# Two products of a channel-mixing layer computed by Strassen's scheme

## The chip, the core and the metric

The kernel runs on one core of one Trainium2 chip. The metric is the device time of one execution in microseconds (us); a kernel's time is the median of its runs.

The engines of the core work side by side, each through its own list of instructions in order, and wait for each other by semaphores. TensorE (PE) multiplies matrices into PSUM, which the kernel uses as 8 banks of 128 x 512 numbers; the loads of its stationary operand are shown as PEld. VectorE (DVE), ScalarE (ACT) and GpSimd (POOL) do elementwise work; POOL gets no PSUM operand here. SyncE (SP) issues the DMAs.

## The reference

Attention with a window and block summaries gives x (2 batches, 768 tokens, 512 channels). Then come two layers. All numbers are float32.

```
def _moe_ref(x, U, V, w_ch1, w_ch2):                 # the first MoE
    h = x.transpose(0, 2, 1) @ U @ V
    u = x + h.transpose(0, 2, 1)
    return u + np.maximum(u @ w_ch1, 0.0) @ w_ch2    # w_ch1 512 x 2048, w_ch2 2048 x 512

def _moe2_ref(x, mu_k, mu_r, w_k, w_v, w_r):         # the second MoE
    x_prev = np.concatenate([zeros, x[:, :-1, :]], axis=1)
    xk = mu_k * x + (1.0 - mu_k) * x_prev
    xr = mu_r * x + (1.0 - mu_r) * x_prev
    k = np.maximum(xk @ w_k, 0.0)                    # w_k 512 x 1024
    v = k * k @ w_v                                  # w_v 1024 x 512
    r = 1.0 / (1.0 + np.exp(-(xr @ w_r)))            # w_r 512 x 512
    return r * v
```

## The kernel before

Every large product runs on PE in the type float32r, with each operand split into a high part (a copy rounded to that type, on ACT) and a low part (the number less its high part, on DVE or POOL). A product is then three matmuls into one bank: high by high, high by low, low by high. So "12 matmuls" below are 4 slices of the contraction x 3.

The weights come as float64 words and are converted on the chip, block by block (128 rows, 512 numbers): `conv_stages` gives nine steps of a block, `load` (SP), `low_words` and `high_words` (ACT), `clamp`, `shift`, `sign` (DVE), `join` (POOL, L407), `high` (ACT, L439), `low` (POOL, L443). There are 54 blocks: 2 for U and V, 16 each for w1 and w2, 8 for wk, 4 for wr, 8 for wv.

The tokens are four chunks of 384 (2 batches x 2). The first part, up to 106 us, attention and the first quarter of the first MoE for batch 0, are an order written out by hand: `ORDER`, a list of step names with numbers that the kernel plays one after the other. A step issues its instructions to their engines, so the list fixes the order within every engine.

After that, generators take over. The first MoE goes by four quarters of its 2048 hidden channels, then chunks, then 4 blocks: `f1` (L483, 12 matmuls of 384 columns), `f2` (L510, 12 matmuls), summed into y (L522). A queue `side` holds jobs of the other engines, above all the conversions of the next weights; `run` takes a job from it at a fixed rate per PE step.

The second MoE, the last 170 us, goes chunk by chunk in `p2_unit`. `prep_jobs` mixes the tokens with their predecessors (L608, L613) and splits them (L619, L624). `k_stage` computes one block of 128 hidden channels: 12 matmuls of 384 columns (L662), relu on ACT (L665), square on DVE (L666), split (L669, L670). `v2_stage`, two blocks later, multiplies the block into three banks, 9 matmuls of 512 columns (L684); with the eighth block the banks are multiplied by the gate (L690, DVE) and stored (L691). `r_stage` computes a gate: 12 matmuls of 512 columns (L646) and a sigmoid (L649), three a chunk. So there are 32 calls each of `k_stage` and `v2_stage` and 12 of `r_stage`. PSUM is two rings of four banks there (`bank`); in `ORDER` the banks are taken and given back one by one (`take`, `give`).

Of the kernel before, what the change touches and what calls it, by code (L numbers as in the profile page):

```python
# [70 lines left out]


# [18 lines left out]
def build(tc, I, out):  # L91
# [241 lines left out]
    def u_stage(n, c):  # L333
        b, d = divmod(n, 4)
        if d == 0:
            u_t[b, c] = (
                pools["u", b].tile([128, KD, CH], F32R, name="uhi", tag="u"),
                pools["u", b].tile([128, KD, CH], F32R, name="ulo", tag="u"),
            )
# [77 lines left out]
    def conv_jobs(blocks, queue=nc.sync):  # L417
        load, *ops = conv_stages(blocks, queue)
        stages = (ops[:2], ops[2:5], ops[5:6], ops[6:7], ops[7:])
        n_blocks = len(blocks)  # L420

        def slot(k):
            if k % 2 == 0 and k // 2 < n_blocks:
                load(k // 2)
            for j in range(len(stages) - 1, -1, -1):
                i, odd = divmod(k - j - 2, 2)
                if not odd and 0 <= i < n_blocks:
                    for op in stages[j]:
                        op(i)

        return [lambda k=k: slot(k) for k in range(2 * n_blocks + len(stages))]
# [16 lines left out]
    def block(nm, f, key, pool, eng=nc_p):
        return (I[nm].bitcast(I32)[f], *put_w(key, pool, eng))

    def quarter_blocks(q, pool):
        res = []
        for i in range(FT):
            f = q * FT + i

            res.append(block("w1", f, ("w1", f), pool, nc_v if q == 0 and i > 1 else nc_p))
            res.append(block("w2", f, ("w2", f), pool))
        return res

# [416 lines left out]
```

## Time and profile before

| | |
|---|---|
| median of 3 runs | 518.05 us (516.36 to 518.37) |
| the profiled execution | 517.4 us |
| its span, first to last instruction | 515.6 us |
| busy PE, DVE, ACT, POOL | 502.8, 320.2, 251.5, 200.6 us |
| granted PE clock | 1.00 throughout (the 2.4 GHz level) |
| moved by DMA | 46.31 MB, mean 90 GB/s |

Span and busy times are of one execution. The matmuls are pipelined: a record's length reaches into the next ones, and what one costs is read from the distance of two starts. PEld is the weight load that belongs to a matmul. A line such as L662 is a line of the kernel above; `bank` is a PSUM bank. "<-" in brackets names what ended an engine's idle time.

### The profile page before, as it was taken

Reading aid. Unit: us, or ns where it says so; the run is one execution under the profiler, and the core shown is the slowest. Engines: PE = TensorE matmul, PEld = TensorE weight load, DVE = VectorE, ACT = ScalarE, POOL = GpSimd, SP = SyncE. Lnnn points to the kernel's source line nnn. Section 1 sums busy time; section 2 is a strip of 40 time slices with the busy share of each in tenths; the row PEclk is TensorE's granted clock in tenths of the full one; section 3 lists DMA queues with packets and bytes.
Section 4 is the critical chain, followed back from the end, with each engine's and each line's share of the span. In section 5 each row is a group of like instructions: output and inputs, shape, how many; then the busy total and the mean of one; then the engine's idle time right before and its main releaser. Section 6 shows DMA issues by size and latency. Waiting matters only on the chain.

```text
span 515.6 us, 8902 instructions
## 1 busy us (share of the span) xinstructions
PE 502.8 (98%) x3468; PEld 467.9 (91%) x3468; DVE 320.2 (62%) x702; ACT 251.5 (49%) x532; POOL 200.6 (39%) x186
## 2 busy tenths in 40 slices
PE   6899999999999999999999999999999999999997
PEld 5578989899999999999999999999878889889885
DVE  6879986458646888368983667476767425343212
ACT  4999866345524454245542546334585424432221
POOL 6547441015634777447783452152621110120000
PEclk9999999999999999999999999999999999999999
DMA  8997651302412333223331230021001001001001
GB/s 312 301 280 228 233 115 49 95 29 95 164 42 81 122 107 102 80 83 123 101 112 73 83 123 1 28 96 47 36 1 61 1 1 63 0 1 38 24 0 61
DMA packets 16329, 46.31 MB, mean 90 GB/s; under 512 B 2704, under 2 KB 4112, under 8 KB 16288
## 3 DMA queue, kind: packets, MB, share of 16 engines
q1 hardware_dynamic: 16112, 45.52, 27.0%
q8 instruction: 27, 0.44, 0.3%
q10 hardware_dynamic: 144, 0.18, 0.1%
q14 instruction: 14, 0.11, 0.1%
q0 software_dynamic: 32, 0.05, 0.0%
HBM read 42.00 MB, written 3.15 MB: 88 GB/s over the span
## 4 chain that ended last, share of the span: by engine, by line
PE 91%; DMA 3%; ACT 2%; DVE 2%; POOL 1%; issue 1%; SPq 0%; DVEq 0%; POOLq 0%
PE bank L510 23%; PE bank L483 22%; PE bank L662 13%; PE bank L684 12%; PE bank L646 5%; PE bank L554 3%; PE bank L578 3%; DMA vt<-vt 2%; PE bank L244 2%; PE bank L289 2%; PE bank L273 2%; PE bank L342 1%; PE bank L311 1%; DMA qt<-qt 1%; PE bank L346 1%
## 5 line engine op out<-in xcount | busy, mean ns | idle before, releaser
L407 POOL TENSOR_TENSOR A<-C,A 128x512 int32<-128x512 int32 (+1 forms) x54 | 70.8, 1310 | 113.3 <-DVE A L401 89.9
L443 POOL TENSOR_TENSOR wlo<-A,whi 128x512 fp32r<-128x512 f32 x50 | 71.3, 1425 | 33.2 <-ACT whi L439 33.2
L510 PE MATMUL bank<-hh,whi 128*128 128x384 f32 x224 | 75.9, 339 | 0.6 <-DVE y L522 0.6
L510 PE MATMUL bank<-hh,wlo 128*128 128x384 f32 x224 | 75.8, 338 | 0.0
L510 PE MATMUL bank<-hl,whi 128*128 128x384 f32 x224 | 75.8, 338 | 0.0
L483 PE MATMUL bank<-uhi,whi 128*128 128x384 f32 x224 | 75.4, 337 | 0.0
L483 PE MATMUL bank<-uhi,wlo 128*128 128x384 f32 x224 | 75.4, 336 | 0.0
L483 PE MATMUL bank<-ulo,whi 128*128 128x384 f32 x224 | 75.4, 336 | 0.0
L490 DVE SCALAR_TENSOR_TENSOR hl<-bank,hh 128x384 fp32r<-128x384 f32 x56 | 31.1, 556 | 67.2 <-ACT hh L488 67.1
L666 DVE TENSOR_TENSOR kt<-kt 128x384 f32<-128x384 f32 x32 | 20.4, 636 | 64.9 <-ACT kt L665 64.9
L488 ACT ACTIVATE hh<-bank 128x384 fp32r<-128x384 f32 x56 | 27.3, 487 | 61.7 <-PE bank L483 61.6
L439 ACT CAST whi<-A 128x512 fp32r<-128x512 f32 x52 | 32.3, 621 | 40.7 <-POOL A L407 40.4
L384 ACT ACTIVATE A<-stg 128x512 f32<-128x512 uint32 (+1 forms) x54 | 36.3, 672 | 29.1 <-DMA stg<-w 16.6
L401 DVE SCALAR_TENSOR_TENSOR A<-stg,A 128x512 int32<-128x512 int32 (+1 forms) x54 | 50.1, 928 | 0.0
L397 DVE TENSOR_SCALAR C<-C 128x512 int32<-128x512 int32 (+1 forms) x54 | 43.6, 808 | 1.7
L662 PE MATMUL bank<-xkl,whi 128*128 128x384 f32 x128 | 43.2, 338 | 0.6 <-POOL xkl L624 0.6
L510 PEld LDWEIGHTS bank<-hh,whi 128*128 128x128 f32 x224 | 42.0, 188 | 1.4 <-ACT C L387 0.9
L662 PE MATMUL bank<-xkh,whi 128*128 128x384 f32 x128 | 43.2, 337 | 0.0
L662 PE MATMUL bank<-xkh,wlo 128*128 128x384 f32 x128 | 43.1, 337 | 0.0
L483 PEld LDWEIGHTS bank<-ulo,whi 128*128 128x128 f32 x224 | 42.1, 188 | 0.0
L483 PEld LDWEIGHTS bank<-uhi,whi 128*128 128x128 f32 x224 | 42.1, 188 | 0.0
L510 PEld LDWEIGHTS bank<-hh,wlo 128*128 128x128 f32 x224 | 42.1, 188 | 0.0
(120 smaller groups left out, 1084.3 us busy)
## 6 DMA issues: line engine op xcount, KB each, us to landing
stg<-w SPq DMA_DIRECT2D x32, 512.0 KB, 3.2
stg<-wk SPq DMA_DIRECT2D x8, 512.0 KB, 3.2
stg<-wv SPq DMA_DIRECT2D x8, 512.0 KB, 3.2
vcat<-vw SPq DMA_DIRECT2D x7, 585.0 KB, 5.3
kt<-kt SPq DMA_DIRECT2D x8, 384.0 KB, 6.2
vt<-vt SPq DMA_DIRECT2D x8, 384.0 KB, 4.7
out<-sig SPq DMA_DIRECT2D x12, 256.0 KB, 2.1
qt<-qt SPq DMA_DIRECT2D x7, 384.0 KB, 6.5
```

What stands on the lines that cost most here:

```text
L384: nc_s.activation(tmp(i, "A"), st[i]["raw"][:, :, 0].bitcast(U32), AF.Copy, scale=2.0 ** -51, bias=2.0)
L397: nc_v.tensor_scalar(out=c, in0=c, scalar1=3, scalar2=None, op0=ALU.logical_shift_left)
L401: nc_v.scalar_tensor_tensor(out=a, in0=st[i]["raw"][:, :, 1], scalar=-2 ** 31, in1=a, op0=ALU.bitwise_and, op1=ALU.bitwise_or)
L407: nc_p.tensor_tensor(out=a, in0=c, in1=a, op=ALU.add)
L439: nc_s.copy(wt[key][0], w)
L443: eng.tensor_tensor(out=lo, in0=w, in1=hi.bitcast(F32), op=ALU.subtract)
L483: nc_t.matmul(ps, w[:, sl], x[:, k], start=(n == 0), stop=(n == 3 * KD - 1))
L488: nc_s.activation(hh, ps, AF.Relu)
L490: lambda: nc_v.scalar_tensor_tensor(out=hl, in0=ps, scalar=0.0, in1=hh.bitcast(F32), op0=ALU.max, op1=ALU.subtract)
L510: nc_t.matmul(acc[d], w[:, sl], x, start=(i == 0 and n == 0), stop=(i == FT - 1 and n == 2))
L662: nc_t.matmul(ps, w[:, sl], x[:, k], start=(n == 0), stop=(n == 3 * KD - 1))
L684: nc_t.matmul(acc, x[:, sl], w, start=(f == 0 and n == 0), stop=(f == KFT - 1 and n == 2))
```

## The change

The products xk @ w_k and k*k @ w_v are computed by Strassen's scheme (in Winograd's form), one level deep. Each operand is cut into 2 x 2 quadrants. For k the cuts go through the hidden channels, the 512 channels of the contraction, and between the two batches; for v through the tokens (the batches), the 1024 hidden channels and the 512 outputs. Seven products of quadrants or sums of quadrants stand for eight. They are numbered 1, 2, 6, 7, 4, 5, 3 in the order in which they run; `LEFT`, `RIGHT` and `RIGHT_X` say which operand each takes ("t" is a scratch quadrant), and the `..._SUMS` tables say how the sums are made, in place.

`k_prod` is one product for one chunk of 384 tokens and one of 4 blocks of 128 hidden channels: 6 matmuls of 384 columns. `k_take` adds its bank to a quadrant z in SBUF (DVE), `k_copy` copies the first one (ACT); product 5 is added twice. `square` and `square_act` do relu and square (one DVE or two ACT instructions, 768 columns). `v_prod` is one product for 128 of 768 rows: 12 matmuls of 256 columns; `v_take` and `v_copy` collect the banks in the same way. Each product needs its operands split anew: a weight quadrant (1024 columns), two pieces of x (768 columns each) or four of z (768 columns each). `gate` multiplies 256 columns, on DVE (`g`) or POOL (`gp`); a store is 128 x 256.

All r products are computed ahead of their use: six (batch 0) before the k products, six (batch 1) after the first two of them.

The generators, `side` and `run` are gone. From the end of `ORDER` on, a second list, `ORDER2` (1198 steps), fixes the order of every engine. Its names: `cl ca cb cc cs cg cp ch co` the nine steps of a conversion; `fa fh fl fb fy yr` the first MoE; `xa xb` mixing; `rh rl ra rs` the gate; `wks xs ms wvs` sums, `wkh xh mh wvh` high parts, `wkl xl ml wvl` low parts; `ka va` products; `kb` to `kg`, `ku` and `vb` to `vg`, `vu` the additions of a product; `q`, `qa` squares; `so` stores. A `p` behind a name puts a step on POOL instead of DVE; the first number of a product is its number in the scheme. The matmuls of the first MoE are the same in number and shape. The blocks of wk and wv are no longer split when converted; `join` writes them into a quadrant. SBUF is laid out by hand in `SLOTS` and `PLACE`; the split parts of z (`mo`) alternate between two pairs of slots.

```diff
+ORDER2 = """
+cl10 fa0.1.0.0 fa0.1.0.1 fh0.1.0.0 cl11 ca10 fl0.1.0.0 cb10 cg10 cc10 fb0.1.0.0 cs10 fh0.1.0.1 cp10 fl0.1.0.1
+cb11 cl12 ca11 cc11 ch10 fa0.1.0.2 cs11 cg11 co10 ca12 cl13 cb12 cg12 fb0.1.0.1 fh0.1.0.2 cp11 fl0.1.0.2 cc12
...
+kr1.2 rlp1.1.2 rl1.1.1 rh1.1.3 ka2.0.0 kr1.3 rl1.1.3 ka2.0.1 kb0.0 wks2 ka2.0.2 kb0.1 ka2.0.3 wksp4 wkh6 kb0.2
+cc51 ka2.1.0 ka2.1.1 kb0.3 ka2.1.2 kb1.0 kb1.1 qa0.0 wkl6 ka2.1.3 ra1.0 kb1.2 xh6.0 kb1.3 xh6.1 cs51 xl6.0
+cp51 wkh7 cg52 ra1.1 rs1.0 xlp6.1 cc50 ra1.2 rs1.1 wklp7 cs50 ra1.3 xh7.0 q0.1 cp50 xh7.1 q0.2 rs1.2 xlp7.0
+ca53 ra1.4 rs1.3 q0.3 cb52 cb53 xlp7.1 ra1.5 cg53 rs1.4 cc52 cs52 ka6.0.0 rs1.5 cc53 cp52 wkh4 cs53 ka6.0.1
+xh4.0 ka6.0.2 kc0.0 cp53 xh4.1 kc0.1 wkl4 ka6.0.3 ka6.1.0 xl4.1 ka6.1.1 kc0.3 kc1.0 ka6.1.2 xl4.0 kc1.1
+ka6.1.3 kc1.2 kc0.2 ka7.0.0 xh5.0 kc1.3 xh5.1 xl5.0 ka7.0.1 wkh5 xlp5.1 kd0.0 ka7.0.2 kd0.1 ka7.0.3 kd0.2
+wklp5 ka7.1.0 kd0.3 ka7.1.1 kd1.0 ka7.1.2 kd1.1 ka7.1.3 kd1.2 ka4.0.0 kd1.3 wkh3 ka4.0.1 xh3.0 ke0.0 wklp3
+xh3.1 ka4.0.2 ke0.1 xl3.1 ka4.0.3 xlp3.0 wvh2 ka4.1.0 ke0.2 ke0.3 ka4.1.1 ke1.0 wvl2 qa1.0 ka4.1.2 ka4.1.3
+ke1.1 mh1.3 ke1.2 ka5.0.0 mh1.2 ml1.3 wvh1 mlp1.2 ke1.3 ka5.0.1 kf0.0 mh1.1 ku0.0 ka5.0.2 kf0.1 mh1.0 ku0.1
+mlp1.1 ka5.0.3 kf0.2 qa1.2 ku0.2 ka5.1.0 kf0.3 ku0.3 mlp1.0 qa1.3 ka5.1.1 kf1.0 ku1.0 ka5.1.2 kf1.1 qa1.1
+wvlp1 ku1.1 ka5.1.3 kf1.2 ku1.2 qa3.0 ka3.0.0 kf1.3 ku1.3 wvsp1 ka3.0.1 kg0.0 mh2.1 ka3.0.2 mh2.0 kg0.1 qa3.3
+ml2.0 ka3.0.3 mlp2.1 ka3.1.0 kg0.2 qa3.1 kg0.3 wvs2 ka3.1.1 qa3.2 wvsp3 ka3.1.2 kg1.1 ka3.1.3 kg1.2 qa2.1
+kg1.0 va1.0 kg1.3 wvs4 qa2.3 va1.1 ms3.1 mh2.3 va1.2 ms3.3 qa2.0 ml2.3 va1.3 mh2.2 ms2.3 va1.4 vr0 ml2.2 qa2.2
+ms3.0 va1.5 vr1 ms2.0 vr4 wvh6 va2.0 ms2.1 vr3 wvl6 vr2 mh6.1 va2.1 mh6.0 vb0 ml6.1 va2.2 mh6.3 vb1 vr5 ml6.0
+wvh7 va2.3 g0.1 ms3.2 so0.1.0 va2.4 ms2.2 ml6.3 mh6.2 va2.5 g0.0 ml6.2 so0.0.0 mh7.3 vb3 va6.0 wvl7 mh7.0
+mh7.1 ml7.3 va6.1 mh7.2 vc0 ml7.0 va6.2 wvh4 ml7.2 va6.3 vb2 g0.3 gp0.2 vb5 so0.3.0 vc1 va6.4 gp0.5 vc2
+so0.2.0 vb4 ml7.1 so0.5.0 gp0.4 va6.5 vc3 vc4 wvl4 so0.4.0 va7.0 mh4.1 ms4.3 mh4.0 mlp4.1 va7.1 vc5 mh4.2 vd0
+ml4.0 mh4.3 va7.2 wvh5 ml4.2 va7.3 ml4.3 va7.4 ms1.0 vd2 va7.5 vd1 ms1.1 vd4 va4.0 mh5.0 ms1.2 mh5.1 vd5 va4.1
+wvl5 mh5.2 wvh3 ml5.1 va4.2 ml5.2 va4.3 ml5.0 ms1.3 va4.4 ms4.2 mh5.3 ve0 va4.5 ml5.3 gp1.0 ve1 va5.0 vd3
+mh3.2 gp1.1 ve2 so1.0.0 ms4.0 mh3.3 so1.1.0 va5.1 ml3.3 mh3.0 ml3.2 va5.2 ms4.1 va5.3 ve3 mh3.1 wvl3 va5.4
+ml3.0 ml3.1 va5.5 ve4 vf1 gp1.4 vf0 va3.0 vu1 gp3.1 so1.4.0 ve5 vu0 gp3.0 so1.1.1 vf3 va3.1 g3.3 gp1.5 so1.0.1
+vu3 so1.3.1 vg0 g1.2 so1.5.0 va3.2 vf2 so1.2.0 g1.3 gp3.2 vf4 so1.3.0 vu4 va3.3 gp3.4 vg1 so1.2.1 vu2 vg2
+so1.4.1 g2.0 va3.4 g2.1 so0.0.1 vg3 so0.1.1 g2.2 gp2.3 vf5 so0.2.1 va3.5 vu5 gp3.5 vg4 so0.3.1 gp2.4 so1.5.1
+vg5 so0.4.1 g2.5 so0.5.1
+"""
...
+SLOTS = {
+    "back": {
+        "A": 3072, "B": 3072, "C": 2048, "U0": 3072, "U1": 3072, "V0": 3072, "V1": 3072, "Y0": 3076
+    },
+    "m": {"D": 4096, "E": 2048, "F": 2048, "Y1": 3076, "R1": 1024, "X1": 1152, "X2": 1536},
+    "n": {"N0": 4096, "N1": 2048, "N2": 1024},
+}
...
+for _p, _n in enumerate((1, 2, 6, 7, 4, 5, 3)):
+    for _i in range(4):
+        PLACE[f"mo{_n}{_i}"] = (("U1", "V0", "Y0", "U0")[_p % 2 * 2 + _i // 2], 1536 * (_i % 2), 1536, 1)
...
+    homes = {tag: (back, n, tag) for tag, n in SLOTS["back"].items()}
+    homes.update({f"H{i}": (h_p, 2 * CH, "h") for i in range(3)})
+    homes.update({f"S{i}": (st_p, 1024, "stg") for i in range(2)})
+    now = {}
+
+    def at(name, n=0, k=0, dt=F32):
+        tag, o, size, *wide = PLACE[name]
+        kind = F32R if wide else F32
+        if tag not in now or now[tag][1] != kind:
+            pool, cols, shared = homes[tag]
+            now[tag] = pool.tile([128, cols], kind, name=tag, tag=shared), kind
+        n = n or size
+        t = now[tag][0][:, o + k * n:o + (k + 1) * n]
+        return t if dt == kind else t.bitcast(dt)
 
...
+            if len(blocks[i]) == 2:
+                to = blocks[i][1]().bitcast(I32)
+                c, a = (t.rearrange("p (h c) -> p h c", h=2) for t in (c, a))
+                del st[i]
+            else:
+                to = a
+            nc_p.tensor_tensor(out=to, in0=c, in1=a, op=ALU.add)
 
...
+    LEFT_SUMS = (((2, 2, 3), ALU.add), (("t", 3, 0), ALU.subtract), ((0, 0, 2), ALU.subtract), ((1, 1, "t"), ALU.subtract))
+    RIGHT_SUMS = (
+        ((0, 1, 0), ALU.subtract), (("t", 3, 0), ALU.subtract), ((1, 3, 1), ALU.subtract), ((2, 2, "t"), ALU.subtract)
+    )
+    X_SUMS = (((1, 1, 0), ALU.subtract), ((0, 0, "t"), ALU.add), (("t", 3, 1), ALU.subtract), ((2, 2, 0), ALU.subtract))
+    LEFT = {1: 0, 2: 1, 6: "t", 7: 0, 4: 3, 5: 2, 3: 1}
+    RIGHT = {1: 0, 2: 2, 6: "t", 7: 1, 4: 2, 5: 0, 3: 3}
+    RIGHT_X = {1: 0, 2: 2, 6: 0, 7: "t", 4: 2, 5: 1, 3: 3}
+
...
+    def sums(eng, table, j, part, *key):
+        places, op = table[j - 1]
+        o, x, y = (part(*key, i) for i in places)
+        eng.tensor_tensor(out=o, in0=x, in1=y, op=op)
+
+    def split_high(dst, src):
+        nc_s.copy(dst[0], src)
+
+    def split_low(eng, dst, src):
+        eng.tensor_tensor(out=dst[1], in0=src, in1=dst[0].bitcast(F32), op=ALU.subtract)
+
...
+    def k_prod(p, c, f):
+        held = k_t[p, c, f] = take()
+        whi, wlo = pair(f"wk{p}")
         n = 0
+        for k in range(2):
+            xhi, xlo = (x[:, c * CH:(c + 1) * CH] for x in x_pair(p, k))
+            sl = slice(f * 256 + k * 128, f * 256 + (k + 1) * 128)
+            for w, x in ((whi, xhi), (whi, xlo), (wlo, xhi)):
+                nc_t.matmul(held[0][:, 0:CH], w[:, sl], x, start=(n == 0), stop=(n == 5))
                 n += 1
+
+    def k_take(p, to, add, last, c, f):
+        held = k_t[p, c, f]
+        z, old = (at(f"z{i}{f}")[:, c * CH:(c + 1) * CH] for i in (to, add))
+        nc_v.tensor_tensor(out=z, in0=held[0][:, 0:CH], in1=old, op=ALU.add)
+        if last:
+            give(held)
+
+    def k_copy(c, f):
+        held = k_t[1, c, f]
+        nc_s.copy(at(f"z1{f}")[:, c * CH:(c + 1) * CH], held[0][:, 0:CH])
+        give(held)
+
+    def square(i, f):
+        z = at(f"z{i}{f}")
+        nc_v.scalar_tensor_tensor(out=z, in0=z, scalar=0.0, in1=z, op0=ALU.max, op1=ALU.mult)
+
+    def square_act(i, f):
+        z = at(f"z{i}{f}")
+        nc_s.activation(z, z, AF.Relu)
+        nc_s.activation(z, z, AF.Square)
+
+    def v_prod(p, s):
+        held = v_t[p, s] = take()
+        whi, wlo = pair(f"wv{p}")
+        n = 0
+        for f in range(4):
+            xhi, xlo = (x[:, s * 128:(s + 1) * 128] for x in pair(f"mo{p}{f}"))
+            sl = slice(f * 256, (f + 1) * 256)
+            for x, w in ((xhi, whi), (xlo, whi), (xhi, wlo)):
+                nc_t.matmul(held[0][:, 0:256], x, w[:, sl], start=(n == 0), stop=(n == 11))
+                n += 1
+
+    def v_copy(s):
+        nc_s.copy(at(f"o1{s}"), v_t[1, s][0][:, 0:256])
+        give(v_t[1, s])
+
+    def o_part(i, s):
+        return at(f"o{i}{s if i else s % 2}")
+
+    def v_take(p, to, add, last, s):
+        held = v_t[p, s]
+        nc_v.tensor_tensor(out=o_part(to, s), in0=held[0][:, 0:256], in1=o_part(add, s), op=ALU.add)
+        if last:
+            give(held)
+
+    def gated(b, s, d):
+        return at(f"sig{b}", DM, s)[:, d * 256:(d + 1) * 256]
+
+    def gate(eng, i, s):
+        t = gated(*((0, s, 0), (1, s, 0), (0, s, 1), (1, s, 1))[i])
+        eng.tensor_tensor(out=t, in0=o_part(i, s), in1=t, op=ALU.mult)
+
+    def store(b, s, d):
+        nc.sync.dma_start(out=out[b, s * 128:(s + 1) * 128, d * 256:(d + 1) * 256], in_=gated(b, s, d))
...
+    steps.update({
+        "fa": f1, "fh": relu_high, "fl": relu_low, "fb": f2, "fy": y_sum, "yr": y_rest,
+        "xa": mix_first, "xb": mix_second, "rh": mix_high, "ra": r_stage, "rs": r_sig,
+        "wkh": lambda p: split_high(*wk_split(p)), "wvh": lambda p: split_high(*wv_split(p)),
+        "xh": lambda *a: split_high(*x_split(*a)), "mh": lambda *a: split_high(*z_split(*a)),
+        "ka": k_prod, "kr": k_copy, "q": square, "qa": square_act, "va": v_prod, "vr": v_copy, "so": store,
+    })
+    for nm, *how in (("b", 2, 0, 1, 1), ("c", 6, 2, 1, 1), ("d", 7, 3, 2, 1), ("e", 4, 1, 3, 1), ("f", 5, 3, 3, 0),
+                     ("u", 5, 2, 2, 1), ("g", 3, 2, 2, 1)):
+        steps["k" + nm] = lambda *a, how=how: k_take(*how, *a)
+        steps["v" + nm] = lambda *a, how=how: v_take(*how, *a)
+    both("rl", mix_low)
+    both("wks", lambda e, j: sums(e, LEFT_SUMS, j, w_part, "wk"))
+    both("wvs", lambda e, j: sums(e, RIGHT_SUMS, j, w_part, "wv"))
+    both("xs", lambda e, j, k: sums(e, X_SUMS, j, x_part, k))
+    both("ms", lambda e, j, k: sums(e, LEFT_SUMS, j, z_part, k))
+    both("wkl", lambda e, p: split_low(e, *wk_split(p)))
+    both("wvl", lambda e, p: split_low(e, *wv_split(p)))
+    both("xl", lambda e, *a: split_low(e, *x_split(*a)))
+    both("ml", lambda e, *a: split_low(e, *z_split(*a)))
+    both("g", gate)
+    play(ORDER2)
```

## Rows read from the trace of the kernel before

**Rows 1.** The page: busy us (share of the span) and instructions of each engine.

```profile
PE 502.8 (98%) x3468; PEld 467.9 (91%) x3468; DVE 320.2 (62%) x702; ACT 251.5 (49%) x532; POOL 200.6 (39%) x186
```

**Rows 2.** The page: shares of the chain that ended last, by engine, by line.

```profile
PE 91%; DMA 3%; ACT 2%; DVE 2%; POOL 1%; issue 1%; SPq 0%; DVEq 0%; POOLq 0%
PE bank L510 23%; PE bank L483 22%; PE bank L662 13%; PE bank L684 12%; PE bank L646 5%; PE bank L554 3%; PE bank L578 3%; DMA vt<-vt 2%; PE bank L244 2%; PE bank L289 2%; PE bank L273 2%; PE bank L342 1%; PE bank L311 1%; DMA qt<-qt 1%; PE bank L346 1%
```

**Rows 3.** Stretches: us, busy PE, PEld, DVE, ACT, POOL, granted clock, DMA.

```profile
340.90:511.60 170.70, 170.13 (x829) 150.08 (x827) 78.27 (x128) 70.41 (x138) 29.19 (x23) 1.00 0.07 24
200.00:250.00 50.00, 50.00 (x287) 49.77 (x286) 34.72 (x52) 21.17 (x39) 30.08 (x25) 1.00 0.28 95
```

**Rows 4.** The chain in order of time: start, us, engine, line, instructions.

```profile
443.21 2.08 PE bank L662 x12
...
500.58 2.12 PE bank L662 x12
502.70 2.10 PE bank L684 x9
504.80 2.79 PE bank L646 x12
```

**Rows 5.** Groups by line, shapes apart: count, busy us, mean ns, idle before.

```profile
L662 PE MATMUL bank<-xkh,whi 128*128 128x384 f32 x128 | 43.2, 337 | 0.0
...
L684 PE MATMUL bank<-whi,hh 128*128 128x512 f32 x96 | 37.9, 395 | 0.0
...
L522 DVE TENSOR_TENSOR y<-bank,y 128x384 f32<-128x384 f32 x48 | 23.3, 548 | 0.0
```

**Rows 6.** PE and its weight loads in order of time: start us, us, instruction.

```profile
60.41 0.60 PE L273 MATMUL bank<-ident,P 128*120 128x128 f32 x4
...
300.16 0.34 PE L483 MATMUL bank<-uhi,whi 128*128 128x384 f32 x1
300.17 0.19 PEld L483 LDWEIGHTS bank<-ulo,whi 128*128 128x128 f32 x1
300.34 0.34 PE L483 MATMUL bank<-ulo,whi 128*128 128x384 f32 x1
```

**Rows 7.** Line L273: durations in ns, smallest, median, largest.

```profile
L273 PE MATMUL bank<-ident,P x96: 270/273/466, 7.3 to 94.9; 128*120 128x128 f32 x96
```

**Rows 8.** DVE in order of time.

```profile
192.57 1.94 DVE L522 TENSOR_TENSOR y<-bank,y 128x384 f32<-128x384 f32 x4
...
356.60 0.69 DVE L401 SCALAR_TENSOR_TENSOR A<-stg,A 128x512 int32<-128x512 int32 x1
357.20 0.42 DVE L391 TENSOR_SCALAR C<-C 128x512 f32<-128x512 f32 x1
...
359.85 1.38 DVE L666 TENSOR_TENSOR kt<-kt 128x384 f32<-128x384 f32 x1 [0.19 <-ACT kt L665]
...
408.15 0.56 DVE L666 TENSOR_TENSOR kt<-kt 128x384 f32<-128x384 f32 x1 [1.99 <-ACT kt L665]
...
409.77 0.55 DVE L624 TENSOR_TENSOR xrl<-xt,xrh 128x384 fp32r<-128x384 f32 x1
```

**Rows 9.** POOL in order of time.

```profile
359.51 1.31 POOL L443 TENSOR_TENSOR wlo<-A,whi 128x512 fp32r<-128x512 f32 x1 [0.73 <-ACT whi L439]
...
402.41 1.01 POOL L624 TENSOR_TENSOR xkl<-xt,xkh 128x384 fp32r<-128x384 f32 x1 [4.96 <-ACT xkh L619]
409.75 1.44 POOL L624 TENSOR_TENSOR xrl<-xt,xrh 128x384 fp32r<-128x384 f32 x1 [6.33 <-ACT xrh L619]
```

**Rows 10.** DMA issues on SP's queue, and the last gates on DVE.

```profile
2.59 0.92 SPq L161 DMA_DIRECT2D kt<-kt  x2
...
510.43 2.15 DVE L690 TENSOR_TENSOR sig<-bank,sig 128x512 f32<-128x512 f32 x3 [5.40 <-PE bank L684]
511.15 1.79 SPq L691 DMA_DIRECT2D out<-sig  x3
```

More of the change, by code (lines that the diff above doesn't have):

```diff
@@ L73, in mask_const @@
+for _i in range(6):
+    PLACE[f"o0{_i}"] = (("E", 1792, 256), ("N2", 768, 256))[_i % 2]
+    PLACE[f"o1{_i}"] = ("E", 256 * _i, 256)
+    PLACE[f"o2{_i}"] = ("C", 256 * _i, 256)
+    PLACE[f"o3{_i}"] = ("F", 768 + 256 * _i, 256) if _i < 5 else ("E", 1536, 256)
 def mask_const():
@@ L335, in u_stage @@
         if d == 0:
[L336 to L339, printed above, removed]
+            u_t[b, c] = [
+                at(f"u{b}{c}", KD * CH, i, F32R).rearrange("p (k c) -> p k c", k=KD) for i in range(2)
+            ]
         ps, _ = ps_t["U", n, c] = take()
@@ L372, in load @@
             src = blocks[i][0]
-            t = (st_p if not wide or i % 3 else x_p).tile([128, 1024], I32, name="stg")
+            if i % 3 == 0 and i < 10:
+                t = x_p.tile([128, 1024], I32, name="stg")
+            else:
+                t = st_p.tile([128, 1024], I32, name="stg", tag="stg")
             p, n = src.shape
-            queue.dma_start(out=t[0:p, 0:n], in_=src)
+            nc.sync.dma_start(out=t[0:p, 0:n], in_=src)
             st[i] = {"raw": t[0:p, 0:n].rearrange("p (n w) -> p n w", w=2), "pn": (p, n // 2)}
@@ L412, in low @@
         def low(i):
-            blocks[i][2](st.pop(i)["A"])
+            blocks[i][2](st[i]["A"])
         return load, low_words, high_words, clamp, shift, sign, join, high, low
[L417 to L431, printed above, removed]
@@ L448, in block, with quarter_blocks @@
[L448 to L458, printed above, removed]
+        return I[nm].bitcast(I32)[f], hi_part, lo_part
+    def quarter_blocks(q, area):
+        return [
+            block(
+                nm, q * FT + i, *(f"{area}{4 * i + 2 * j + k}" for k in range(2)),
+                nc_v if q == 0 and i > 1 and nm == "w1" else nc_p,
+            )
+            for i in range(FT) for j, nm in enumerate(("w1", "w2"))
+        ]
@@ L503, in f2 @@
-        acc = acc_t[q, b, c]
+            acc_t[q, b, c] = [take() for _ in range(KD)]
         for d in range(KD):
-            if d == 2:
-                hold[0] = i == FT - 1
-                yield
             sl = slice(d * 128, (d + 1) * 128)
@@ L642, in r_stage @@
+    def r_stage(b, s):
+        held = r_t[b, s] = take()
+        c, o = divmod(s * 128, CH)
         n = 0
@@ L812, in build @@
-    drain(side)
-    for n, (b, c) in enumerate(chunks):
-        gen = p2_unit(b, c)
-        if n == 0:
-            next(gen)
-            ffn_flush()
-        if n == 0:
-            side.extend(conv_jobs([block("wr", k, ("wr", k), wb_p) for k in range(KD)]))
-        if n + 1 < len(chunks):
-            side.extend(prep_jobs(*chunks[n + 1], mix))
-        run(gen, 1.3 if n == 0 else 0.7)
-        drain(side)
-    while waiting:
-        v2_stage(*waiting.popleft())
+        first_blocks += quarter_blocks(q, ("wa", "wb")[q % 2])
```

402 lines of the change are left out of this document (179 added, 223 removed), and 9 rows, old and new, of the table PLACE.

## The prediction

> **What bounds the kernel now.** I read the page's busy shares first: TensorE (PE) is busy 98% of the span, VectorE (DVE) 62%, GpSimd (POOL) 39% [rows 1]. A busy PE is not yet a bound, so the chain of waits comes next: 91% of the chain that ended last is PE, and the lines of the k product (L662, 13%) and the v product (L684, 12%) have the shares that they have of the work [rows 2]. The table by stretches says the same of the place that changes: from 340.9 to 511.6 us, where r, k and v are computed, PE is busy 170.1 of 170.7 us at full granted clock (1.00, the 2.4 GHz level), while DVE is busy 78.3 and POOL 29.2 [rows 3]. So here every matmul taken off PE is worth its spacing, as long as nothing else becomes late; and the other engines have room, DVE about half.
>
> A matmul's record (337 ns for 384 columns, 395 for 512) overlaps its neighbours [rows 5], so it is not the price. The price is the distance from start to start: the chain gives 12 matmuls of L662 in 2.08 to 2.12 us (174.5 ns each), 9 of L684 in 2.10 us (233 ns), 12 of L646 in 2.79 us (232.5 ns) [rows 4]. Both are 0.454 ns a column.
>
> **Matmuls removed and added.** k before: 4 chunks x 8 blocks x 12 = 384 matmuls of 384 columns, three groups of 128 [rows 5]. k after: `k_prod` has 2 x 3 matmuls, 7 products x 2 chunks x 4 blocks = 56 calls, 336 matmuls of the same width. 48 x 174.5 ns = 8.4 us less.
>
> v before: 288 of 512 columns, three groups of 96 [rows 5], 67.1 us at 233 ns. v after: `v_prod` has 4 x 3 matmuls, 7 x 6 = 42 calls, 504 of 256 columns. No row shows 256 columns. In proportion it is 256 x 0.454 = 116 ns. From below the nearest row is the transposes of L273, 128 columns with a new weight tile each: four take 0.60 us, one record is 0.273, so they are 109 ns apart although half as much streams [rows 6, 7]; there the weight load is what spaces them, and every one of the 504 has a load of the same size. From above the nearest row is 384 columns, 174.5 ns. The load can lie under the stream: the load for the next matmul starts with the matmul before it (300.17 beside 300.16), and the next matmul starts 0.18 us on [rows 6]. I take 116 ns, which is just above the 110: 58.5 us, 8.6 less than before (55.4 and 87.9 at the two ends: 11.7 less or 20.8 more).
>
> That load speaks against the change, and so does the Trainium skill. "TensorE: Matmul & The Clock Gate", section "The mechanism", says that a weight load overlaps a running matmul only when the two use different row groups; here all use the whole array. By that rule and the page's estimate of 107 ns for a 128-column load, load and stream would add up to about 213 ns, 504 of them 107 us, and the v products would be 40 us slower. The rows of 384 columns disagree: by the rule they would be some 267 ns apart, and are 174.
>
> PE alone: 515.6 - 8.4 - 8.6 = 498.6 us of span. The r products (144 matmuls) and the first MoE keep their matmuls.
>
> **What it puts on the other engines.** Prices are again from start to start. DVE: four PSUM additions of 384 columns take 1.94 us with the last record at 0.55, so 0.465 each; a 512-column operation on SBUF 0.60 (L401 at 356.60, next at 357.20) [rows 8]. The slope gives 0.33 for 256 columns, 0.87 for 768, 1.14 for 1024. POOL: 1.01 for 384 columns, 1.31 for 512 when it runs first [rows 9], so 0.72 for 256, 1.9 for 768, 2.5 for 1024.
>
> The second thing the traces show is that POOL and a DVE operation with two SBUF inputs exclude each other. L666 takes 0.56 us alone; started at 359.85 behind a POOL subtraction that ran from 359.51 for 1.31, it took 1.38, the rest of POOL's time and then its own [rows 8, 9]. It goes the other way too: at 409.75 POOL's 1.01 became 1.44, with DVE's 0.55 inside it. DVE additions from PSUM (L522) are not stretched: mean 548 ns over all 48 [rows 5].
>
> Now the counts from ORDER2, by stage. *Stage v (va1.0 to the end), PE 42 x 12 x 0.116 = 58.5 us.* DVE: 42 `v_take` x 0.33 = 13.9 and one k addition 0.5 (PSUM); 21 low parts and 16 sums x 0.87 = 32.2; 5 weight low parts and 1 sum x 1.14 = 6.8; 10 gates x 0.33 = 3.3. Together 56.7 us, 97% of PE's time. POOL: 14 gates x 0.72 + one low part 1.9 = 12.0 us, in which 42.3 of DVE's 56.7 us may not run. If half of POOL's time falls beside PSUM additions or waits, DVE needs 62.7: 4.2 us more than PE's 58.5. *Stage k after ra1 (ka6 to ka3), PE 41.9 us.* DVE 31.2, of which 21.9 from PSUM; POOL 26.2. Sum 57.4; if 60% of the PSUM part lies beside POOL, 44.3, 2.4 over. Inputs of a product are made about one product (8.4 us) ahead here, so this lag costs PE nothing at first, but stage v takes it over. *Stage ra0 to ra1 (50.2 us)*: DVE 25.0, POOL 28.8, sum 53.8 less the overlap of 5.6 us of PSUM additions: even, and with a lead of several us before ka6 needs its parts.
>
> Why lag in stage v reaches PE: the halves `mo` of a product lie in one of two slots, so `mh7` (ACT) and `ml7` (DVE) can't begin before va2 has ended, and all four must be ready when va6 has, 8.4 us later, the first matmul of a product wanting f=0 and its twelfth f=3. Four low parts are 3.5 us of DVE; the list puts up to 5 us of additions, sums and weight parts between them. DVE runs in order: a low part that is late holds the `v_take` behind it, and these hold PSUM banks. At va1 to va2 it is closest, since `mh2.2`, `mh2.3` need the slot that ka3 reads, and squares on ACT (`qa`, two passes) stand before them.
>
> I charge 5 us in all for PE waiting in stage v (bounds 0, if the additions always fall beside POOL, and 16: all of POOL's 12.0 on top of DVE, 68.7 - 58.5 = 10.2, the 2.4, and some 3 us of waits at product changes).
>
> **Edits at nothing.** The conversions of the weights keep their count (54 blocks), only their order moves; 16 blocks lose `ch` and `co`, and their POOL time becomes the sums. In the first MoE, PE was fully busy with the old side jobs (50.00 of 50.00, DVE 34.7, POOL 30.1 from 200 to 250: 65 us of the two in 50) [rows 3]; by the prices above the new list gives DVE 8 to 10.5 us and POOL 9 to 13 in each chunk of 16.7 us of the second and third quarter, about the same, so I cost it at 0, and at most 2 us if a low part of h comes behind a POOL operation. The tail: three gates at the end take 2.15 us and three stores follow [rows 10]; after, one addition, one gate, a half-size store, but POOL's last gate may stand before it: 0, or 1 either way. The stores become 24 on SP's queue, 16 of them in va3; two issues of a load take 0.92 us there [rows 10], so 16 are 7.4 of 8.4 us: 0, unless the gates come in a bunch at the end (1 us).
>
> **Sum.** 498.6 + 5 = 503.6 us of span. The profiled execution took 517.4 us for a span of 515.6, so 1.8 around it; 505.4. The median of the runs is 518.05, 0.65 above that execution: 506.
>
> **Rivals.**
> (a) *All of it is kept.* DVE's additions hide beside POOL and PE never waits: 498.6 + 1.8 + 0.6 = 501, or 498 at 110 ns a matmul. For it: the first MoE already runs DVE and POOL at 65 of 50 us together with PE full [rows 3]. Against: there the products of an engine are wanted tens of us later, here within one product. 0.2.
> (b) *Most is given back.* DVE sets the pace of stage v and its lag from stage k comes on top, 10 to 16 us of waits: 511 to 517. For it: 97% load on an in-order engine that also waits for ACT and PE. 0.16.
> (c) *Slower: the weight load shows.* Place: the 504 matmuls of `v_prod`. If the load needs more than the stream of 256 columns hides, the spacing rises; the change breaks even at 116 + 17.0/504 = 150 ns. At the 174.5 ns of 384 columns v costs 87.9, span 528.0, time 530; with load and stream one after the other (110 + 116) 114 us, time about 556. For it: 110 ns where half as many columns stream, 6 ns under my price. Against: the same share of 9% above a column per cycle at 384 and 512 columns, which no load bound would give. 0.09.
> (d) *It doesn't do what it says*, because the second MoE wasn't bound by PE: excluded by 170.1 of 170.7.
>
> **How the numbers follow.** Mine 0.55 (502 to 510), (a) 0.2, (b) 0.16, (c) 0.09. Half a per cent, 2.6 us, is about what a measurement of this kernel can tell from no change. Faster by more than that (below 515.4): mine, (a), and most of (b), 0.85, less something for delays that I can't see in a list of 1198 steps: 0.82. Within: 0.08. Slower: (c), 0.10. The range reaches to the far end of (a) and through (b): 498 to 517, leaving out (c) and some 8 in 100 more at its two ends.
>
> **What would show it.** PE's matmul count falls from 3468 to 3468 - 48 + 216 = 3636. Twelve matmuls of 256 columns stand 1.39 us apart in the chain; 1.8 or more would be (c). The k calls of six stand 1.05 us apart. In stage v DVE is busy above 90% by records, PE shows waits of 0.5 to 2 us at product changes (va1 to va2 above all), put down to DVE's low parts, and DVE's two-input records are stretched where POOL runs. No such waits is (a); waits inside products, on banks, is (b). The prediction is wrong if PE waits appear in the first MoE or at ka6.

## The result: 499.5 us, and the profile after

The changed kernel takes 499.5 us (median of 4 runs, 498.3 to 500.9) where the kernel before takes 518.2 (4 runs beside it): a ratio of 0.9648, 95% interval 0.9613 to 0.9682. I had predicted 506, with 498 to 517 as the range. The direction is right; the 5 us that I let DVE take back are not there, and what came is the rival in which all of it is kept (501).

The profiled execution has a span of 498.1 us. The page's first part (busy us, share, instructions), answering to [rows 1]:

```profile
PE 484.7 (97%) x3636; PEld 464.1 (93%) x3636; DVE 401.4 (81%) x790; ACT 276.2 (55%) x532; POOL 252.3 (51%) x203
```

3636 matmuls, as counted. DVE, POOL and ACT do 81, 52 and 25 us more. The page's shares of the chain that ended last, answering to [rows 2]:

```profile
PE 79%; DVE 10%; ACT 6%; DMA 3%; issue 1%; SPq 0%; DVEq 0%
```

PE's share fell from 91 to 79%, and DVE has 10%, ACT 6%. The chain in order of time (start, us, line, instructions) says where; it answers to [rows 4]. L707 is r, L772 `k_prod`, L804 `v_prod`; L742 are low parts, L739 high parts and L736 sums; L778 and L816 are the additions of k and v, L793 and L794 the two passes of `square_act`, L825 the gates, L828 the stores. The letters are slots of SBUF.

```profile
341.94 16.79 PE bank L707 x72
358.74 16.80 PE bank L772 x96
375.54 16.78 PE bank L707 x72
392.32 18.89 PE bank L772 x108
...
415.83 0.85 ACT H L794
416.69 1.46 ACT V L739 x2
...
439.71 0.96 DVE U L742
440.67 0.88 DVE B L736
...
483.10 1.81 DVE U L742 x2
...
485.39 8.73 PE bank L804 x72
```

r and the first k products run on PE without a break: 96 matmuls of 384 columns in 16.80 us are 175 ns each. From 415.0 to 439.7 us the chain goes through ACT's squares and high parts, from 439.7 to 485.4 through DVE, and then it returns to PE. A chain that runs through ACT and DVE says that they were just in time or late. They were late at one place: the only wait of PE above 0.2 us after the first part of the program is at 485.4, at the first matmul of va3 (engine, line, what it waited for: us, times, longest us):

```profile
PE bank L804 <- DVE E L816: 0.5, 1, 0.5
```

The stretches of stage k (after the second r), of the first product of stage v, and of all of stage v, answering to [rows 3] (length, then busy PE, PEld, DVE, ACT, POOL, granted clock, DMA):

```profile
391.90:434.00 42.10, 42.10 (x242) 42.02 (x241) 38.52 (x61) 27.90 (x35) 29.47 (x14) 1.00 0.00 1
...
434.20:442.60 8.40, 8.40 (x74) 8.40 (x73) 8.07 (x11) 8.30 (x13) 0.38 (x1) 1.00 0.00 0
...
434.10:494.10 60.00, 59.50 (x505) 59.14 (x503) 58.84 (x95) 29.18 (x40) 14.02 (x16) 1.00 0.13 45
```

In stage v DVE is busy 58.8 of 60.0 us and PE 59.5: a tie. In its first product ACT is tied too, with 8.3 of 8.4 us. The price of 256 columns, which no row of before had, from PE in order of time:

```profile
489.71 0.86 PE L804 MATMUL bank<-N,U 128*128 128x256 f32 x6
490.41 0.87 PE L804 MATMUL bank<-N,V 128*128 128x256 f32 x6
491.12 0.86 PE L804 MATMUL bank<-N,U 128*128 128x256 f32 x6
```

Twelve take 491.12 - 489.71 = 1.41 us, 117.5 ns each; 504 of them 59.2 us. Last, the end, answering to [rows 10]:

```profile
494.15 0.42 DVE L816 TENSOR_TENSOR C<-bank,C 128x256 f32<-128x256 f32 x1 [0.57 <-PE bank L804]
...
494.61 0.42 DVE L825 TENSOR_TENSOR V<-C,V 128x256 f32<-128x256 f32 x1
494.65 0.81 SPq L828 DMA_DIRECT2D out<-V  x2
```

One addition, one gate, a store: from PE's last matmul to the end 4.0 us, as before.

Where the 17.5 us of span came from, by the starts of PE's lines in the two traces (a k call that the kernel before runs ahead of its last `f2` is counted to the second MoE): the first part (to the first `f1` matmul) 106.3 before, 107.3 after; the first MoE 236.7 and 234.6, 2.1 won; the second MoE 168.6 and 152.2, 16.4 won; the tail 4.0 and 4.0. The 1.0 us lost in the first part can't be put down to the change: its steps are the same in the changed kernel and in all the runs below, and in these twelve traces it ends anywhere from 105.8 to 110.3 us.

### The profile page after: what moved, and what is told of

It reads as the page before. It is cut to its first block, busy times and chain, and to the rows that moved or that the text cites. A ratio compares the mean times of both kernels' runs of the same rounds, so it can differ in the third digit from the quotient of the medians.

```text
span 498.1 us, 9378 instructions
## 1 busy us (share of the span) xinstructions
PE 484.7 (97%) x3636; PEld 464.1 (93%) x3636; DVE 401.4 (81%) x790; ACT 276.2 (55%) x532; POOL 252.3 (51%) x203
## 4 chain that ended last, share of the span: by engine, by line
PE 79%; DVE 10%; ACT 6%; DMA 3%; issue 1%; SPq 0%; DVEq 0%
PE bank L595 24%; PE bank L618 23%; PE bank L772 7%; PE bank L707 7%; PE bank L640 4%; PE bank L663 4%; DMA vt<-vt 3%; PE bank L370 2%; PE bank L415 2%; DVE U L742 2%; PE bank L399 2%; PE bank L804 2%; PE bank L467 1%; DVE N L742 1%; DVE V L742 1%; PE bank L437 1%
## 5 line engine op out<-in xcount | busy, mean ns | idle before, releaser
L605 DVE SCALAR_TENSOR_TENSOR h<-bank,h 128x384 fp32r<-128x384 f32 x56 | 30.9, 552 | 45.0 <-ACT h L600 44.7
L600 ACT ACTIVATE h<-bank 128x384 fp32r<-128x384 f32 x56 | 27.4, 488 | 68.1 <-PE bank L595 68.1
L519 DVE TENSOR_SCALAR C<-C 128x512 f32<-128x512 f32 (+1 forms) x54 | 43.7, 810 | 3.3 <-POOL A L541 2.0
L515 ACT ACTIVATE C<-stg 128x512 f32<-128x512 f32 (+1 forms) x54 | 36.2, 673 | 7.6 <-POOL N L541 5.6
L804 PE MATMUL bank<-N,U 128*128 128x256 f32 x252 | 35.9, 280 | 0.5 <-DVE E L816 0.5
L618 PE MATMUL bank<-h,D 128*128 128x384 f32 x192 | 35.9, 336 | 0.0
L618 PEld LDWEIGHTS bank<-h,D 128*128 128x128 f32 x192 | 33.5, 188 | 0.0
L393 ACT ACTIVATE P<-P,nm 128x120 f32<-128x120 f32 x96 | 29.6, 385 | 6.9 <-DVE nm L382 6.7
L804 PEld LDWEIGHTS bank<-N,U 128*128 128x128 f32 x252 | 32.5, 188 | 0.7 <-issue 0.7
L618 PE MATMUL bank<-h,B 128*128 128x384 f32 x144 | 27.2, 337 | 0.0
L707 PE MATMUL bank<-N,U 128*128 128x512 f32 x108 | 27.1, 395 | 0.0
L707 PEld LDWEIGHTS bank<-N,U 128*128 128x128 f32 x108 | 20.2, 188 | 4.7
L804 PE MATMUL bank<-N,V 128*128 128x256 f32 x144 | 21.0, 282 | 0.0
```

Source lines behind the costliest of these rows:

```text
L515: nc_s.activation(tmp(i, "C"), st[i]["raw"][:, :, 1].bitcast(F32), AF.Abs)
L519: nc_v.tensor_scalar(out=c, in0=c, scalar1=as_float(0x38000000), scalar2=as_float(0x47EFFE00), op0=ALU.max, op1=ALU.min)
L605: nc_v.scalar_tensor_tensor(out=hl, in0=held[0][:, 0:CH], scalar=0.0, in1=hh.bitcast(F32), op0=ALU.max, op1=ALU.subtract)
L618: nc_t.matmul(acc_t[q, b, c][d][0][:, 0:CH], w[:, sl], x, start=(i == 0 and n == 0), stop=(i == FT - 1 and n == 2))
L707: nc_t.matmul(held[0], xr(c, i)[:, k, o:o + 128], w, start=(n == 0), stop=(n == 3 * KD - 1))
L804: nc_t.matmul(held[0][:, 0:256], x, w[:, sl], start=(n == 0), stop=(n == 11))
```

## The experiments

All are the changed kernel with one thing altered, and stand against its 499.5 us (499.49 where it was run again, beside the run with both sets of matmuls and the one without POOL's gates). The kernel before took 518.1 to 518.2 beside each of them. "..." marks a cut in the code.

**Put the k matmuls back.** 49 of the 56 k calls repeat their last matmul.

```diff
+        last = 5 if (c, f) == (1, 3) else 6
...
+        if last == 6:
+            nc_t.matmul(held[0][:, 0:CH], wlo[:, sl], xhi, start=False, stop=True)
```

> Of the 48 matmuls that the k products lost, 49 are put back: each of 49 of the 56 k calls gets a seventh matmul of 384 columns, a repeat of its last one, so its sum holds that term twice. Nothing else moves. Theory 1, PE sets the time in stage k and the fewer matmuls are the gain: 49 x 174.5 ns = +8.5 us, 508.0 from 499.5. Theory 2, the gain of the k products came from somewhere else, the new list or the removed squares on the old path: PE has hidden room in stage k and the time stays within 2 us of 499.5. Rival with the engines tied: DVE, busy 38.3 of 41.9 us there, gets the extra 8.5 us as slack, so stage v starts with its low parts further ahead and the time grows by 7.5 at most 8.5.

Measured 508.8 us, +9.3 (507.2 to 509.8). In the traces it is 83.9 us from the first k matmul to the last, against 75.3, with the second r between them: +8.6, against the 8.5 of the first theory. PE sets the time there.

**Put the v matmuls back.** Two more in 36 of the 42 v calls.

```diff
+        last = 13 if s < 5 or p == 1 else 11
...
+        for _ in range(last - 11):
+            nc_t.matmul(held[0][:, 0:256], xhi, wlo[:, sl], start=False, stop=(n == last))
+            n += 1
```

> 72 matmuls of 256 columns are put back into the v products: two more, repeats of the last one, in 36 of the 42 calls, so these sums hold that term three times; 576 x 256 columns are the 288 x 512 of before. Theory 1, PE sets the time in stage v: 72 x 117 ns = +8.4 us, 507.9. Theory 2, DVE sets the pace in stage v (it is busy 59.1 of 60.3 us there) and PE runs in its shadow: the first extra microsecond of PE is free and the rest is not, +7 to +7.5 us, 507; if DVE were the bound by more than its busy time shows, much less, 500 to 503.

507.6 us, +8.1, and PE's one wait is gone. The runs (506.6 to 509.5) can't tell the theories' +8.4 from +7.5. The traces can: from the first v matmul to the last it is 67.6 us in place of 59.7, +7.8, which is 72 matmuls at 117.5 ns (8.5) less the 0.6 us that PE had lost in stage v to waits. PE was the bound there too, DVE not above it by more than that.

**Both at once**, with the changed kernel run again beside it.

> The changed kernel as it is, as the base for the other two runs of this call: 498 to 501 us.

> Both sets of matmuls are put back at once (49 of 384 columns into the k products, 72 of 256 into the v products, each a repeat of a term that the sum then holds more than once), with all else of the change left in. Theory 1, the fewer matmuls of PE are the gain of the second MoE, and the rest of the gain is the first MoE's (236.7 to 234.6 us of span): 8.6 + 8.4 = +17.0, so 516.5 if the base is 499.5, some 2 us below the kernel before. Theory 2, one of the two hides in room that the other makes: +10 to +14, 510 to 514.

499.49 and 516.1 us: +16.6. This kernel has the new list, Strassen's sums and all the added work of DVE, POOL and ACT, and PE streams as many columns as before the change (384 more): it is 0.9953 of the kernel before (0.9933 to 0.9973). In the traces its second MoE is 16.4 us longer than that of the changed kernel, which is all that the change had won there. So nearly the whole gain is the matmuls, and the remaining 2.1 us are as much as the first MoE won in the trace.

**Double seven DVE operations in stage v.**

```diff
-... ml2.3 ... ms2.3 ... ml6.1 ... ml7.3 ... ml4.0 ... ml5.1 ... ml3.3 ...
+... ml2.3 ml2.3 ... ms2.3 ms2.3 ... ml6.1 ml6.1 ... (and so on)
```

> Seven DVE operations of 768 columns in stage v are done twice (six low parts and one sum, the same values written again): 7 x 0.87 = 6.1 us more DVE work, none of it a product's last input. Theory 1, PE alone sets stage v and DVE has room: 0 to +1 us, 499.5 to 500.5. Theory 2, the two are tied at 98%: DVE has 60.3 - 59.1 = 1.2 us left, the rest shows: +4.5 to +6 us, 504 to 505.5. The charge in my prediction (DVE 4 to 5 us over PE) would need the full 6.1, 505.6.

506.5 us, +7.0 (505.6 to 510.1). In the stretch of stage v DVE is busy 65.5 of 66.5 us, and PE waits five times, for 4.3 us, three times for DVE and twice for a high part of ACT:

```profile
452.68 0.38 PE L804 MATMUL bank<-N,V 128*128 128x256 f32 x1 [0.84 <-ACT V L739]
...
453.90 1.25 PE L804 MATMUL bank<-N,V 128*128 128x256 f32 x5 [0.83 <-DVE V L742]
...
492.00 0.96 PE L804 MATMUL bank<-N,U 128*128 128x256 f32 x6 [1.61 <-DVE E L816]
```

Every microsecond of the 6.1 showed: the tie is real, DVE has nothing to spare. In the trace the second MoE is 6.6 us longer, and DVE's busy time in stage v grew by as much; the rest of the +7.0 is within the spread of the runs. The mean granted clock of that stretch is 0.97, where it was 1.00.

**Leave out 12 sums.**

```diff
-... ms3.1 ... ms3.3 ... ms1.0 ... ms4.2 ...    (all ms1, ms3, ms4)
```

> 12 of the 16 sums of z are left out (all but zt = z3 - z0), so the v products take other operands than the scheme wants; 12 x 0.87 = 10.4 us of DVE work less in stage v. Theory 1, PE sets stage v and DVE is tied with it: only the waits of PE go, 0.3 + 0.6 us of 60.3, so 498.6 to 499.5. Theory 2, DVE paces stage v by more than PE's idle shows: 494 to 497.

498.0 us, 1.5 less. DVE is busy 47.0 us in this stretch, and PE all of it:

```profile
434.20:492.60 58.40, 58.40 (x500) 58.40 (x499) 47.03 (x82) 28.09 (x40) 13.44 (x15) 1.00 0.14 47
```

12 us less work on DVE buy 1.5, of which the trace shows 0.7 in stage v (from the first v matmul to the last 59.0 us for 59.7): DVE's excess over PE was no more than that.

**Move POOL's gates to DVE, and leave them out.** The first changes `gp` to `g` in the list, the second deletes the 14 steps.

> The 14 gates of POOL run on DVE, at the same place of the list: 14 x 0.33 = 4.6 us more on DVE, and POOL has only one operation left in stage v (1.9 us). If POOL's 12 us cost DVE half of themselves, as I charged, DVE wins 5 or 6 us back and the time stays at 499.5. If they cost it 2.4 us (59.1 busy less the 56.7 of the sum), DVE needs 59.1 + 4.6 - 2.0 = 61.7 of 60.3: +1 to +2.5 us, 500.5 to 502.

> The 14 gates of POOL are left out, so 14 of the 24 output blocks are not multiplied by r. DVE's list stays as it is, and POOL has 1.9 us of work in stage v in place of 12. If POOL blocked DVE for half of its time, DVE would win 5 us and PE would lose its last waits: 498 and DVE busy about 54 us in stage v. If POOL's gates ran beside DVE's additions from PSUM, 498.5 to 500 and DVE busy 57 to 59.

On DVE: 503.9 us, +4.4, with 4.6 us of work moved; stage v grew by 1.3 us in the profiled execution and the tail by 2.2. (That execution is the longest of the four, 506.4 us; 3.0 of its excess lie in the first part.) Left out: 499.3 us. The stretch of stage v without POOL's gates, of the same length as the one of after:

```profile
433.00:493.00 60.00, 59.48 (x505) 59.11 (x503) 58.76 (x96) 29.17 (x40) 2.65 (x2) 1.00 0.14 47
```

POOL is busy 2.65 us in place of 14.0, and DVE 58.76 in place of 58.84. So POOL's gates cost DVE 0.1 us. Both of my expectations for the move to DVE missed: I had still credited it with 2 us or more of blocking taken away, and there was next to none to take.

**Double seven DVE low parts in stage k.**

```diff
-... wkl4 ... xl4.1 ... xl4.0 ... xl5.0 ... xl3.1 ... ml1.3 ... ml2.0 ...
+... wkl4 wkl4 ... xl4.1 xl4.1 ... (and so on)
```

> The same dose in stage k, ka6 to ka3: seven low parts on DVE are done twice, six of 768 columns and one of 1024, 6.4 us more. DVE is busy 38.3 of 41.9 us there, part of it waiting for POOL. Theory 1, inputs are a product ahead, so the lag is absorbed: 0 to +1 us, 500. Theory 2, the lag is handed on to stage v, which has about 1 us to spare: 6.4 - 3.6 - 1.2 = +1.6 us or more, 501 to 503; with POOL in the way of the longer DVE list up to +6, 505.

511.8 us, +12.3, with seven runs from 508.9 to 516.3: nearly twice the 6.4 us of the dose, and beyond both theories. The reason is in two views of this run. DVE and then POOL in order of time:

```profile
402.50 4.82 DVE L742 TENSOR_TENSOR U<-A,U 128x768 fp32r<-128x768 f32 x2
...
435.36 5.37 DVE L742 TENSOR_TENSOR Y<-H,Y 128x768 fp32r<-128x768 f32 x2
```

```profile
401.63 1.85 POOL L742 TENSOR_TENSOR Y<-V,Y 128x768 fp32r<-128x768 f32 x1 [4.19 <-ACT Y L739]
403.43 3.07 POOL L742 TENSOR_TENSOR C<-N,C 128x1024 fp32r<-128x1024 f32 x1
...
434.98 1.85 POOL L742 TENSOR_TENSOR Y<-H,Y 128x768 fp32r<-128x768 f32 x1
436.80 3.12 POOL L736 TENSOR_TENSOR D<-D 128x1024 f32<-128x1024 f32 x1
```

Two low parts that take 1.82 us alone take 4.82 and 5.37 where POOL is running. The list was in step: POOL's operations lay for the most part beside DVE's additions. Pushed out of step, four of the doubled low parts wait 10.0 us in all for POOL, where the four single ones waited 0.8. PE then waits 3.3 us in stage k and 4.7 in stage v. The first wait leaves its clock at 1.00; behind two waits that end at 449.8 and 450.8 (1.9 and 0.6 us) it falls:

```profile
400.70:409.10 8.40, 5.10 (x30) 4.76 (x29) 8.37 (x9) 1.74 (x3) 4.87 (x2) 1.00 0.00 0
...
451.00:459.40 8.40, 8.40 (x61) 8.40 (x62) 8.33 (x12) 6.26 (x12) 0.00 (x0) 0.82 0.05 18
```

61 matmuls in 8.4 us, where 74 ran in such a stretch of after. In the trace the second MoE is 10.4 us longer than in after, 7.4 of it in waits of PE, so the slower clock has a share in the price too. (The profiled execution, 510.1 us, is one of the shorter of the seven.)

**The same dose without the collision.** In stage k, 14 additions from PSUM are done twice; the first of the two keeps the bank.

```diff
+        steps["zk" + nm] = lambda *a, how=how: k_take(*how[:3], 0, *a)
...
-... kc0.0 ... kd0.1 ...
+... zkc0.0 kc0.0 ... zkd0.1 kd0.1 ...
```

> In stage k, 14 additions from PSUM are done twice (the same sum written again): 14 x 0.465 = 6.5 us more on DVE, as much as the seven low parts done twice, which took +12.3 us (511.8). Theory 1, those cost double because they need two SBUF inputs and wait for POOL: these don't, so DVE is only 6.5 us later, with 3.6 us free in stage k and 1.2 in stage v: +2 to +5 us, 501.5 to 504.5. Theory 2, any delay of DVE there costs that much, since PE waits for banks: +10 us or more, 510.

503.9 us, +4.4. A pair takes 1.06 us in the trace, so the dose is 14 x 0.6 = 8.3 us, more than the low parts' 6.4, and it costs a third as much. PE waits 3.5 us in place of 8.0; the mean granted clock of stage v is 0.97 in both runs. So it is the two SBUF inputs beside POOL that cost, not the delay alone.

**Split the v matmuls.** Each of 256 columns becomes two of 128, each with its own weight load.

```diff
-        for f in range(4):
...
+        for o in (0, 128):
+            n = 0
+            for f in range(4):
...
+                sl = slice(f * 256 + o, f * 256 + o + 128)
...
+                    nc_t.matmul(held[0][:, o:o + 128], x, w[:, sl], start=(n == 0), stop=(n == 11))
```

> Each matmul of 256 columns in the v products is issued as two of 128, with the same stationary operand loaded twice; the sums are the same. Theory 1, the weight load spaces matmuls of 128 columns (109 ns between the transposes of the kernel before): 1008 x 109 = 109.9 us against 504 x 117 = 59.1, +50.8 us, 550; the 117 ns of 256 columns are then 8 ns above that floor. Theory 2, the load hides at this width too and 9% above a column per cycle goes on: 58 ns each, stage v unchanged, 499.5 to 501.

553.4 us, +53.9. PE in order of time:

```profile
450.25 0.83 PE L806 MATMUL bank<-N,U 128*128 128x128 f32 x6
450.92 0.83 PE L806 MATMUL bank<-N,Y 128*128 128x128 f32 x6
```

Six in 0.67 us, 111.7 ns each, though only half as much streams as at 117.5. That is a floor under a load and its matmul, close to the 109 ns of the transposes [rows 6], and the change sits 6 ns above it: the products could not be made narrower at a gain.

## Why the prediction was right, and where not

*PE bounds the second MoE, and the matmuls are the gain.* Right: +16.6 us when they are put back, against the 17.0 of the sum.

*The prices.* k: 175 ns, as taken. v: 117.5 ns for 116, so the v products won 67.1 - 59.2 = 7.9 us and not 8.6. The floor at 110 stood where the transposes had put it (111.7). The rule of the Trainium skill in "TensorE: Matmul & The Clock Gate", section "The mechanism", that a weight load overlaps a running matmul only in other row groups, is not what these runs show. 128 columns more take 57.5 ns from 384 to 512 columns, and if load and stream followed each other they would take as much from 128 to 256; there the distance grows by 5.8, all on the whole array. So load and stream overlap, and rival (c), whose break-even was 150 ns, falls. That it is the load which sets the floor, as the prediction says of the transposes, no run shows by itself: every matmul here has a load of its own.

*DVE's work in stage v.* 56.7 us by my sum, 58.8 busy in the trace: the reading "97% of PE's time" was nearly right, and most of the 2.1 us more is one collision with POOL.

*POOL in DVE's way.* This is the step that failed: "If half of POOL's time falls beside PSUM additions or waits, DVE needs 62.7". It charges DVE with all of the other half, 6.0 us. DVE paid 1.9. DVE and then POOL in order of time, in stage v of the changed kernel:

```profile
457.64 0.95 DVE L742 TENSOR_TENSOR Y<-B,Y 128x768 fp32r<-128x768 f32 x1
...
460.31 2.60 DVE L736 TENSOR_TENSOR F<-F,C 128x768 f32<-128x768 f32 x1
```

```profile
457.80 1.39 POOL L825 TENSOR_TENSOR V<-E,V 128x256 f32<-128x256 f32 x1 [0.23 <-DVE E L816]
459.90 2.19 POOL L742 TENSOR_TENSOR U<-X,U 128x768 fp32r<-128x768 f32 x1 [0.72 <-ACT U L739]
```

The sum of 2.60 us (0.95 alone) waits behind POOL's one low part; that is 1.7 of the 1.9 us, and one sum behind a gate is the rest. The gate of 1.39 us (0.73 alone) started behind a DVE low part, and there it is POOL that waits. By the records of both engines 9.2 of POOL's 14.1 us lie beside additions or beside no work of DVE: two thirds, not far from my half. But the rest is not DVE's alone to pay: where POOL came second its records are stretched, by 2.3 us in all (above 0.72 for a gate and 1.85 for the low part), and POOL had the time. With the 14 gates gone, 11 us of POOL's work, DVE's busy time moved by 0.1.

In stage k it is the order that keeps them apart. The exclusion of [rows 8, 9] exists there, as the doubled low parts show, but I priced it as if the two lists met nearly at random, with 60% of DVE's additions beside POOL. By the records it is 19.1 of 23.8 us, 80%: the order puts POOL's long operations beside runs of additions. In ka5 of the changed kernel, DVE and POOL in order of time:

```profile
418.78 0.55 DVE L778 TENSOR_TENSOR X<-bank,X 128x384 f32<-128x384 f32 x1
419.24 0.55 DVE L778 TENSOR_TENSOR A<-bank,A 128x384 f32<-128x384 f32 x1
419.71 0.55 DVE L778 TENSOR_TENSOR X<-bank,X 128x384 f32<-128x384 f32 x1
...
425.24 0.55 DVE L778 TENSOR_TENSOR N<-bank,N 128x384 f32<-128x384 f32 x1
425.81 0.56 DVE L778 TENSOR_TENSOR S<-bank,S 128x384 f32<-128x384 f32 x1
```

```profile
418.27 1.85 POOL L742 TENSOR_TENSOR V<-B,V 128x768 fp32r<-128x768 f32 x1 [3.07 <-ACT V L739]
420.08 3.69 POOL L742 TENSOR_TENSOR U<-B,U 128x768 fp32r<-128x768 f32 x2
423.71 2.44 POOL L742 TENSOR_TENSOR N<-D,N 128x1024 fp32r<-128x1024 f32 x1
```

From 418.3 to 426.1 POOL is busy almost without a break with four operations of two SBUF inputs, none stretched, and DVE adds one bank after another, none stretched either. ORDER2 says so before any run: between `ka5.0.0` and `ka3.0.0` the DVE steps are, after one low part and one `ke`, only `kf` and `ku`, the POOL steps `mlp` and `wvlp`. I had counted both by stage and not read which stand beside which.

*The lag from stage k, 2.4 us.* Not there: I had DVE at 44.3 us, and it was busy 38.5 of 42.1. Its records there are stretched behind POOL by some 3.5 us in all, but that left room, and no wait of PE follows until va3.

*Waits at product changes.* One of 0.5 us, at va3 and not at va1 to va2, on a bank that an addition still held. The tie of DVE and PE was right; that it would come out 4 us on DVE's side was not.

*The first MoE at nothing.* It gave 2.1 us, the largest reason that the time came out below rival (a)'s 501. In the trace of before PE pauses three times (0.9 us at 177.5 in place of 0.17, less at 228.8 and 296.1), 1.2 us in all; after, there is none. The rest is in the spacing: outside the pauses a matmul stands 175.2 ns from the next before and 174.4 after, 1.0 us over the first MoE. Why is open. The 2.1 us stand on one trace of the list before, against twelve of the new one, which all have 234.5 or 234.6 us; they fit the 2.1 us left over in the run with both sets of matmuls back, and were not tried by themselves.

The tail and SP's queue were right at 0. The sum of 498.6 also kept a pause that PE made before the change in the second MoE (0.8 us at 382.2, where a low part on POOL was late) and that is gone. With 498.6, plus 0.6 for the dearer v matmuls and 0.6 for the waits, less 2.1 in the first MoE and 0.8 for that pause, plus the 1.0 by which the first part of this execution was longer, the span comes to 497.9; it was 498.1.

None of the runs with the whole computation beats the changed kernel: relieving DVE can give 1.5 us at most (the run without sums), and POOL has no more places beside additions that I saw. Relieving ACT, which is as tight in the first product of stage v, was not tried.

## What to carry to other kernels

Where two engines exclude each other, a sum over a stage only bounds the cost; read the order and see which operations stand beside which and which of the two comes second, since that one waits, and waiting was free here on the engine with time to spare. A list that is in step this way can lose more than the work that is added: 6.4 us of work that met POOL cost 12.3, while 8.3 us that did not cost 4.4. And count a matmul from start to start, with a floor from the narrowest one in the trace that loads its own weights.
